# A fused attention and routed-FFN kernel: minima placed behind two-bank maxima, a unit's copy made in halves, attention rows split during the FFN, two late products evicted by ScalarE and GpSimd

## The chip, the cores and the metric

The kernel runs on one core of a Trainium2 chip. The core's engines run side by side, each with its own instruction queue worked off in order: TensorE (PE in the profile; PEld is its weight load) multiplies matrices into PSUM, VectorE (DVE) and ScalarE (ACT) read PSUM and work on it, GpSimd (POOL) works on SBUF, and SyncE (SP) issues nearly all DMA transfers of this kernel. They meet through semaphores only. The metric is the device time of one execution in microseconds; less is better. A verdict needs a difference that a few repeated runs can tell from none.

## The reference: what is computed

The input x has 2048 rows of 512 numbers. Two branches are mixed row by row by a gate:

```python
g = sigmoid((x * gate_w).sum(-1))
a = softmax_attention(x, wqkv, 32 heads of 16) @ wo
b = x, with a SwiGLU FFN added to the 2 rows that score highest in x @ w_r
out = g * a + (1 - g) * b
```

Nearly all the work is the attention: 32 heads, each with a 2048 x 2048 table of scores, its row maximum, its exponentials and its product with V.

## The kernel before: how the work is laid out

**Units and steps.** The attention is cut into 32 units (`UNITS`). A unit is a pair of heads and half of the queries; the last four units take a quarter of the queries of four heads. A unit has 16 steps (`KT`), one for each 128 keys, so there are 512 steps (`STEPS`). A step has four score pieces (`s_piece`, L655): a matmul with the transposed scores into one of three `st` banks of PSUM, and an exponential on ScalarE (L663) into `P`. Two steps later `av_mm` (L665) multiplies `P` with V and adds it up over the 16 steps in the one bank `av`. At the end of a unit `av_out` (L677) copies that bank to SBUF with one ScalarE instruction (L684; for a few units of the end with VectorE, L682) and SyncE sends the rows on.

**Maxima.** Before a unit's scores are exponentiated, the row maxima are needed. `m_piece` (L576) computes the scores once more, with queries as rows, 64 pieces to a unit (`EL`), in groups of three: two pieces fill the two-bank tile `mxa`, the third fills the one-bank tile `mxb`. VectorE reduces `mxa` with one instruction after the second piece (`r == 1`) and `mxb` with one after the third (`r == 2`), both at L590, into negated maxima `Mr`. A unit's 64 pieces do not divide by three, so units end at different places of a group: unit u ends behind a one-bank reduction if u % 3 is 2, behind a two-bank one if u % 3 is 1, and inside a two-bank tile if u % 3 is 0. At the end `m_unit` (L631) takes the minimum of the negated maxima on VectorE (L633) and splits it into a high and a low part on GpSimd (`pool_split`, L76); at the next two-bank reduction `m_rows` (L645) transposes the result on VectorE (L648) and sends it into rows 48 and 49 of the query tile `Qx` with eight small DMAs (L653). The score matmul of the unit then subtracts the maximum by itself. The maxima run 21 steps (`LEAD`) ahead of the exponentials, so a unit's rows are complete about five steps before its first step.

**The order is written out by hand.** One round of the loop (L954 to L973) walks the string `ORDER`, `sssmmA smssmmA msssmmf smssmmAm`: 12 score pieces (three steps), 12 pieces of maxima, three products with V (`A`) and one slot `f` for other work. The round thus has four groups of three pieces of maxima, called segments here: each has one two-bank and one one-bank reduction. `A` counts the steps; as it starts at -2 and a round has three, a unit ends on the third A of a round if u % 3 is 0, on the first if it is 1, on the second if it is 2.

**Other work.** The generator `slots` (L840) fills the `f` slots: the projections of the later heads, the FFN (`ff_in`, `ff_t`, `ff_down`, `ff_sum`), and the output projection with `wo` in three parts: `wo_groups((0, 1), (2,))`, `wo_groups((2,))` and `wo_last` (L564), one slot for each of 16 row tiles t or two. What a slot leaves in the one PSUM bank `fl` is evicted by a function put into the list `late`; `run_late` (L196) runs that list at the start of the next round. For the output projection it is `acc_add` (L471): ScalarE scales the bank into a tile `w` (L474) and GpSimd adds that to the accumulator (L475). `wo_last`, called one slot each for t = 12 to 15 with 64 rows (`k`) and then for t = 0 to 8 with 128, does not use the list: `finish` (L557) does both on VectorE with one instruction (L559), and `store` (L561) sends complete row tiles out. `at_step(s, ...)` puts a call at the end of step s; `gaps` holds small VectorE work, one item of which follows a two-bank reduction when neither `turn` nor anything else is due there.

**Attention rows for the output projection.** `load_at` (L491) reads 256 attention rows back with their reciprocal sums, `split_at` (L498) multiplies and splits them on GpSimd (six instructions for two groups of heads). The first such load stands behind `ff_sum`, and `wait(s + 8)` (L834, L879) leaves `f` slots empty until eight steps later. `load_acc` (L462) brings the residual x back from DRAM behind the scatter of the FFN's rows (L453), and `acc_scale` (L467) multiplies it by 1 - g on GpSimd.

**The end.** The round loop ends when the maxima are complete, with step 491. The 21 steps left run in a plain loop (L974 to L982) with one fill after each product with V. In it, `l_unit` (L729), called at the ends of steps 500 and 503, normalises the rows of unit 30: a reciprocal on VectorE (L733), a store to and a broadcast load from DRAM (L734, L736), a multiplication and the split (`split_last`, L541); `wo_last(8, 128)` waits for step 505 and needs that result of unit 30. After it comes `tail` (L754).

Of the kernel before, what the change touches and what calls it, by code (L numbers as in the profile page):

```python
# [36 lines left out]
def gated_mix(ctx: ExitStack, tc: tile.TileContext, xT, x, wqkv, wo, w_rg, w_gate, w_up, w_down,  # L37
# [526 lines left out]
    def wo_last(t, k):  # L564
        half, tt = divmod(t, 8)
        ah, al = lastp[half]
        ps = fl_tile()
        wo_terms(ps, ah[:k], al[:k], 3, slice(tt * 128, tt * 128 + 128), True, True)
        finish(t, ps)
        if k == 128:  # L570
            store(t)

# [3 lines left out]
    def m_piece(g):  # L576

        u, e = divmod(g, EL)
        t, c, j = e // 8, e // 2 % 4, e % 2
        r = g % 3  # L580
        if r == 0:
            MX[0] = mxa_tile()
        elif r == 2:
            MX[1] = mxb_tile()
        dst = MX[0][:, r] if r < 2 else MX[1]
        nc.tensor.matmul(dst, Qx[u % 3][64 * j:64 * j + 48, t * 128:t * 128 + 128],  # L586
                         k_of(u, t // 4)[64 * j:64 * j + 48, c * 512:c * 512 + 512], start=True, stop=True)
        if r:
            g0 = (g - 1 if r == 1 else g) % (3 * EL)
            nc.vector.tensor_reduce(Mr[:, g0:g0 + (2 if r == 1 else 1)], MX[r - 1], axis=AX.X, op=OP.max, negate=True)  # L590
            if r == 1:

                if turn:
                    m_rows(*turn.pop())
                elif e > 1 and e < EL - 1 and gaps:
                    gaps.pop(0)()
            if e == EL - 1 or (e == 0 and r == 1 and g):
                m_unit(u if e else u - 1)
                if u == UNITS - 1 and e:
                    m_rows(*turn.pop())  # L600
# [39 lines left out]
            pool_split(hl[:, :, 0], hl[:, :, 1], m)  # L640
        turn.append((u, hl))

    turn, gaps = [], []

    def m_rows(u, hl):  # L645

# [8 lines left out]
    def s_piece(s, j, c):  # L655
        u, kt = divmod(s, KT)
        if s not in P:
            P[s] = ring.tile([128, 4, 512], F32, tag="P", name="P", bufs=3)
        k = k_of(u, c)[64 * j:64 * j + 50, kt * 128:kt * 128 + 128]
        q = Qx[u % 3][64 * j:64 * j + 50, c * 512:c * 512 + 512]  # L660
        ps = mxb_tile() if s > STEPS - LEAD and c == 1 and j == 0 else st_tile()
        nc.tensor.matmul(ps, k, q, start=True, stop=True)  # L662
        nc.scalar.activation(P[s][:, 2 * j + c, :], ps, AF.Exp)  # L663

    def av_mm(s):  # L665
        u, kt = divmod(s, KT)
# [8 lines left out]
    Lt = {}  # L675

    def av_out(u):  # L677
        pair, half = divmod(u, 2)
        g, pp = divmod(pair, 4)
        o = o_tile("o", [128, 512])  # L680
        if STEPS > u * KT + KT + 2 > STEPS - LEAD:
            nc.vector.tensor_copy(o, AV[0])  # L682
        else:
            nc.scalar.activation(o, AV[0], AF.Copy)  # L684
        if u >= QU:
            AV[u] = o
            if u == UNITS - 1:
# [113 lines left out]
    def at_step(s, f, *a):  # L801
        fill.setdefault(s, []).append((f, a))
# [37 lines left out]
    def slots():  # L840
# [23 lines left out]
        at_step(now[0] + 3, load_wo)  # L864
        for c in range(4):
            at_step(now[0] + 6 + c, split_wo, c)
        yield
        yield
        yield from ff_down()
# [1 line left out]
        last_tiles()  # L871
        s = now[0]
        for nb in range(4):
            at_step(s + 5 + 2 * nb, load_acc, nb)
        for t in range(16):
            at_step(s + 11 + t, acc_scale, t)
        at_step(s + 1, load_at, 0, (0, 1))
        at_step(s + 4, split_at, 0, (0, 1))
        yield from wait(s + 8)  # L879
        yield from wo_groups((0, 1), (2,))  # L880
        assert now[0] > 3 * 8 * KT + 16
        yield from wo_groups((2,))
# [69 lines left out]
    count["m"] = 4 * LEAD  # L952

    while count["m"] < UNITS * EL:  # L954
        run_late()
        for o in ORDER:
            if o == "s":
                s, i = divmod(count["s"], 4)
# [8 lines left out]
            elif o == "A":  # L967
                if count["A"] < 0:
                    parts_next(2)
                p_v(count["A"])  # L970
                count["A"] += 1
            else:
                next(fills, None)  # L973
    for s in range(count["s"] // 4, STEPS + 2):  # L974
# [45 lines left out]
```

## Time and profile before

| what | value |
|---|---|
| median of 3 runs | 1425.82 us (1425.69 to 1426.97) |
| the profiled execution: time, span | 1426.34 us, 1424.4 us |
| granted TensorE clock | 0.999 |
| VectorE busy | 1292.2 us (91%), 1534 instructions |
| ScalarE busy | 1169.2 us (82%), 2264 instructions |
| GpSimd busy | 318.5 us (22%), 335 instructions |
| DMA | 92.87 MB, mean 65 GB/s |
| exponentials (L663, from `st`) | 2028, 1064.3 us, 599 ns each |
| maxima (L590) | 655 two-bank of 1216 ns, 654 one-bank of 689 ns |
| minima (L633) | 32 of 220 ns |
| copies of a unit (L684) | 31 of 600 ns |
| `finish` (L559), loop and tail | 18 of about 750 ns |
| `acc_add` (L474, L475) | 34 of about 700 ns and 1282 ns |

The span is the time from the first to the last instruction in the trace; the execution's own time has 1.9 us around it. A line of the timeline has the start in us, the duration in us, the engine, the line of the code, the operation and its tiles; in brackets stands how long the engine was idle before, and what ended that. Instructions on one engine overlap by some hundredths of a microsecond, so that starts, not durations, tell the pace.

### The profile page before, as it was taken

The page shows a single profiled execution, that of the slowest core. Times are in us where ns is not written, and L with a number is a line of the kernel's source. Part 1 is how long each engine was busy: PE and PEld are TensorE (multiplying, and loading weights), DVE is VectorE, ACT ScalarE, POOL GpSimd, SP SyncE. Part 2 cuts the span into 40 slices and gives each one's busy share as a digit, 9 for nine tenths or more (in the row PEclk, how much of TensorE's full clock was granted, in tenths as well). Part 3 has the DMA queues.
Part 4 walks back from the last instruction along what each step waited for, and adds up shares of the span by engine and source line. Part 5 has one row for each costly group of instructions (what it writes and reads, how often), then busy time and mean ns, then how long its engine had stood idle before and what let it go on. Part 6 is the DMA issues. An engine that isn't in the chain of part 4 may idle for free.

```text
span 1424.4 us, 24160 instructions
## 1 busy us (share of the span) xinstructions
PE 1416.3 (99%) x9113; PEld 627.8 (44%) x9113; DVE 1292.2 (91%) x1534; ACT 1169.2 (82%) x2264; POOL 318.5 (22%) x335
## 2 busy tenths in 40 slices
PE   9999999999999999999999999999999999999998
PEld 6654444444444444444444443434444444444433
DVE  6889999999999999999999999999999999999942
ACT  5568888888888888888888888888888888888886
POOL 4851101102000001200000100032742322234501
PEclk9999999999999999999999999999999999999999
DMA  8601121212123121312222332414313031012012
GB/s 245 230 27 51 31 40 31 68 31 52 46 67 92 62 53 32 67 31 67 55 83 53 100 87 69 103 40 129 83 31 68 22 76 37 14 31 58 17 49 79
DMA packets 51592, 92.87 MB, mean 65 GB/s; under 512 B 14208, under 2 KB 21376, under 8 KB 49844
## 3 DMA queue, kind: packets, MB, share of 16 engines
q1 hardware_dynamic: 51188, 91.02, 24.1%
q8 instruction: 72, 1.18, 0.3%
q0 software_dynamic: 288, 0.30, 0.1%
q14 instruction: 44, 0.36, 0.1%
HBM read 63.77 MB, written 28.57 MB: 65 GB/s over the span
## 4 chain that ended last, share of the span: by engine, by line
PE 99%; DMA 0%; ACT 0%; DVE 0%; SPq 0%; issue 0%; DVEq 0%; ACTq 0%
PE av L671 36%; PE st L662 24%; PE mxa L586 12%; PE mxb L586 10%; PE fl L154 6%; PE fl L508 4%; PE st L298 3%; PE st L154 2%; PE mxa L617 1%; PE fl L399 1%; DMA xs<-xT 0%; PE fl L437 0%; PE mxb L662 0%; DVE acc L559 0%; ACT P L663 0%; PE mxa L508 0%
## 5 line engine op out<-in xcount | busy, mean ns | idle before, releaser
L663 ACT ACTIVATE P<-st 128x512 f32<-128x512 f32 x2028 | 1064.3, 599 | 199.1 <-PE st L662 109.9
L590 DVE TENSOR_REDUCE Mr<-mxa 128x2 f32<-128x1024 f32 x655 | 796.6, 1216 | 3.3 <-PE mxa L586 2.5
L671 PE MATMUL av<-P,V 128*32 128x512 f32 x4096 | 545.3, 604 | 0.0
L662 PE MATMUL st<-Qx,Kx 50*128 50x512 f32 x2028 | 538.1, 444 | 1.3 <-ACT P L663 1.1
L590 DVE TENSOR_REDUCE Mr<-mxb 128x1 f32<-128x512 f32 x654 | 450.9, 689 | 62.1 <-PE st L662 21.7
L662 PEld LDWEIGHTS st<-Qx,Kx 50*128 50x128 f32 x2028 | 276.5, 184 | 233.6 <-ACT P L663 214.6
L586 PE MATMUL mxb<-Kx,Qx 48*128 48x512 f32 x654 | 325.3, 497 | 0.0
L586 PE MATMUL mxa<-Kx,Qx 48*128 48x512 f32 x1310 | 295.8, 417 | 0.0
L586 PEld LDWEIGHTS mxb<-Kx,Qx 48*128 48x128 f32 x654 | 119.5, 183 | 273.7 <-DVE Mr L590 271.2
L586 PEld LDWEIGHTS mxa<-Kx,Qx 48*128 48x128 f32 x1310 | 124.9, 183 | 46.4 <-DVE Mr L590 5.4
L671 PEld LDWEIGHTS av<-P,V 128*32 128x32 f32 x4096 | 81.1, 108 | 141.3 <-issue 135.2
L77 POOL TENSOR_SCALAR hl<-m 128x16 fp32r<-128x16 f32 x31 | 7.9, 254 | 435.3 <-DVE m L633 435.3
L205 POOL TENSOR_SCALAR ev<-pe 128x512 fp32r<-128x512 f32 x24 | 35.8, 1492 | 299.0 <-ACT pe L203 299.0
L475 POOL TENSOR_TENSOR acc<-acc,w 128x512 f32<-128x512 f32 x34 | 43.6, 1282 | 187.6 <-ACT w L474 173.5
L154 PE MATMUL fl<-xh,wh 128*128 128x512 f32 x96 | 42.9, 447 | 0.0
L154 PE MATMUL fl<-xh,wl 128*128 128x512 f32 x96 | 40.4, 421 | 0.0
L508 PE MATMUL fl<-woh,ahl 128*128 128x512 f32 x96 | 35.1, 447 | 0.0
L622 DVE TENSOR_REDUCE Mr<-mxa 128x2 f32<-128x1024 f32 x21 | 25.7, 1224 | 8.4 <-PE mxa L617 8.4
L154 PE MATMUL fl<-xl,wh 128*128 128x512 f32 x96 | 32.6, 421 | 0.0
L300 ACT ACTIVATE V<-st 128x512 f32<-128x512 f32 x16 | 9.6, 600 | 27.7 <-PE st L298 27.7
L206 POOL TENSOR_TENSOR ev<-pe,ev 128x512 fp32r<-128x512 f32 x24 | 30.8, 1285 | 2.0
L559 DVE SCALAR_TENSOR_TENSOR acc<-fl,gg,acc 128x512 f32<-128x512 f32 x13 | 9.7, 748 | 20.1 <-PE fl L508 17.8
(190 smaller groups left out, 778.6 us busy)
## 6 DMA issues: line engine op xcount, KB each, us to landing
q_scr<-ev SPq DMA_DIRECT2D x15, 512.0 KB
Kx<-k_scr SPq DMA_DIRECT2D x30, 256.0 KB
Qx<-q_scr SPq DMA_DIRECT2D x54, 128.0 KB
k_scr<-ev SPq DMA_DIRECT2D x13, 512.0 KB
Qx<-q_scr SPq DMA_DIRECT2D x70, 64.0 KB
xs<-xT SPq DMA_DIRECT2D x16, 256.0 KB
xn<-x SPq DMA_DIRECT2D x4, 1024.0 KB
Qx<-hr SPq DMA_DIRECT2D x256, 2.0 KB
```

The lines of the kernel that those rows point to most:

```text
L154: nc.tensor.matmul(ps, a[:, i, c, :], b[nb][:, c, :], start=n == 0, stop=n == 11)
L205: nc.gpsimd.tensor_scalar(ev[:, 0], t, 1.0, None, op0=OP.mult)
L206: nc.gpsimd.tensor_sub(ev[:, 1], t, ev[:, 0].bitcast(F32))
L298: nc.tensor.matmul(ps, a[nb][:, c, sl], b[:, c, :], start=c == 0 and n == 0, stop=c == 3 and n == 2)
L475: nc.gpsimd.tensor_add(a, a, w)
L508: nc.tensor.matmul(ps, a[:, sl], b[:a.shape[0], c, :], start=first and n == 0, stop=last and n == 2)
L586: nc.tensor.matmul(dst, Qx[u % 3][64 * j:64 * j + 48, t * 128:t * 128 + 128], k_of(u, t // 4)[64 * j:64 * j + 48, c * 512:c * 512 + 512], ...
L590: nc.vector.tensor_reduce(Mr[:, g0:g0 + (2 if r == 1 else 1)], MX[r - 1], axis=AX.X, op=OP.max, negate=True)
L622: nc.vector.tensor_reduce(*r, axis=AX.X, op=OP.max, negate=True)
L662: nc.tensor.matmul(ps, k, q, start=True, stop=True)
L663: nc.scalar.activation(P[s][:, 2 * j + c, :], ps, AF.Exp)
L671: nc.tensor.matmul(AV[0][32 * ct:32 * ct + 32, :], V[:, kt, h * VW:h * VW + 32], P[s][:, ct, :], start=kt == 0, stop=kt == KT - 1)
```

## The change

- **Minima.** In units that end behind a one-bank reduction (u % 3 is 2) `m_unit` is no longer called at once: the unit's number goes into a new list `due`, and `m_unit` runs behind the next two-bank reduction, two pieces later. `m_rows` then falls on the two-bank reduction after that. These are units 2, 5, ..., 29, ten of them.
- **Copy in halves.** For units that end on the second A of a round (u % 3 is 2, the same ten units) `av_out` copies 256 columns at once, and `o_half` the other 256 after the third exponential that follows. The DMAs of the unit's rows (`o_rows`, the old second part of `av_out`) are issued behind the second half.
- **Held evictions.** In the ten rounds that begin just after the end of a unit (u % 3 is 0), `run_late` runs behind the round's first A instead of at its start.
- **Attention rows during the FFN.** The first `load_at` and `split_at` stand between `ff_t(1)` and `ff_down`, at the fifth and the tenth step after the former. The wait of eight steps is gone, so the output projection starts two rounds earlier and all later fills move up by two slots; `load_acc` and `acc_scale` are placed anew behind `ff_sum`.
- **Late products.** `wo_last` puts `acc_add` into `late` as long as the step is below 490, and uses `finish` from then on. With the fills two slots earlier, `wo_last` for t = 12 and 13 falls on steps 485 and 488, and t = 14 on step 491.

```diff
@@ wo_last
-        finish(t, ps)
+        if now[0] < STEPS - LEAD - 1:
+            late.append((acc_add, (t, ps, gg)))
+        else:
+            finish(t, ps)
         if k == 128:
             store(t)
@@ m_piece
             if r == 1:
 
-                if turn:
+                if due:
+                    m_unit(due.pop())
+                elif turn:
                     m_rows(*turn.pop())
                 elif e > 1 and e < EL - 1 and gaps:
                     gaps.pop(0)()
-            if e == EL - 1 or (e == 0 and r == 1 and g):
+            if e == EL - 1 and r == 2 and u < UNITS - 1:
+                due.append(u)
+            elif e == EL - 1 or (e == 0 and r == 1 and g):
                 m_unit(u if e else u - 1)
@@
-    turn, gaps = [], []
+    due, turn, gaps = [], [], []
@@ s_piece
         nc.scalar.activation(P[s][:, 2 * j + c, :], ps, AF.Exp)
+        o_half()
@@ av_out
     def av_out(u):
-        pair, half = divmod(u, 2)
-        g, pp = divmod(pair, 4)
         o = o_tile("o", [128, 512])
         if STEPS > u * KT + KT + 2 > STEPS - LEAD:
             nc.vector.tensor_copy(o, AV[0])
+        elif STEPS - LEAD > u * KT + KT + 2 and u % 3 == 2:
+            nc.scalar.activation(o[:, :256], AV[0][:, :256], AF.Copy)
+            half_o.append([3, u, o, AV[0]])
+            return
         else:
             nc.scalar.activation(o, AV[0], AF.Copy)
+        o_rows(u, o)
+
+    half_o = []
+
+    def o_half():
+
+        if half_o:
+            half_o[0][0] -= 1
+            if not half_o[0][0]:
+                _, u, o, ps = half_o.pop()
+                nc.scalar.activation(o[:, 256:], ps[:, 256:], AF.Copy)
+                o_rows(u, o)
+
+    def o_rows(u, o):
+        pair, half = divmod(u, 2)
+        g, pp = divmod(pair, 4)
         if u >= QU:
@@ slots
         at_step(now[0] + 3, load_wo)
         for c in range(4):
             at_step(now[0] + 6 + c, split_wo, c)
+        at_step(now[0] + 5, load_at, 0, (0, 1))
+        at_step(now[0] + 10, split_at, 0, (0, 1))
         yield
         yield
         yield from ff_down()
@@
         s = now[0]
         for nb in range(4):
-            at_step(s + 5 + 2 * nb, load_acc, nb)
+            at_step(s + 3 + 3 * nb, load_acc, nb)
         for t in range(16):
-            at_step(s + 11 + t, acc_scale, t)
-        at_step(s + 1, load_at, 0, (0, 1))
-        at_step(s + 4, split_at, 0, (0, 1))
-        yield from wait(s + 8)
+            at_step(s + 6 + t, acc_scale, t)
+        yield
         yield from wo_groups((0, 1), (2,))
@@ the loop
     while count["m"] < UNITS * EL:
-        run_late()
+        hold = count["A"] % KT == 0 and count["A"] > 0
+        if not hold:
+            run_late()
         for o in ORDER:
...
                 p_v(count["A"])
                 count["A"] += 1
+                if hold:
+                    hold = False
+                    run_late()
             else:
                 next(fills, None)
```

## The prediction

> **What bounds the kernel now.** I read the busy times first, then the chain of waits.
>
> ```profile
> PE 1416.3 (99%) x9113; PEld 627.8 (44%) x9113; DVE 1292.2 (91%) x1534; ACT 1169.2 (82%) x2264; POOL 318.5 (22%) x335
> PE 99%; DMA 0%; ACT 0%; DVE 0%; SPq 0%; issue 0%; DVEq 0%; ACTq 0%
> ```
>
> TensorE looks full, but the ends of its matmuls are modelled and a late matmul stays "busy". So neither view tells whether an edit on another engine is worth anything. What does is the pace of the loop, and for that I took VectorE's timeline and measured from the start of one two-bank reduction to the start of the one four segments (a round, three steps) later.
>
> ```profile
> 97.86 1.23 DVE L590 TENSOR_REDUCE Mr<-mxa 128x2 f32<-128x1024 f32 x1 [0.30 <-PE mxa L586]
> ...
> 113.37 1.21 DVE L590 TENSOR_REDUCE Mr<-mxa 128x2 f32<-128x1024 f32 x1
> ...
> 121.08 1.22 DVE L590 TENSOR_REDUCE Mr<-mxa 128x2 f32<-128x1024 f32 x1
> 122.33 0.22 DVE L633 TENSOR_REDUCE m<-Mr 128x16 f32<-128x64 f32 x1
> ...
> 136.53 1.22 DVE L590 TENSOR_REDUCE Mr<-mxa 128x2 f32<-128x1024 f32 x1
> ...
> 159.80 1.22 DVE L590 TENSOR_REDUCE Mr<-mxa 128x2 f32<-128x1024 f32 x1
> ...
> 163.77 0.22 DVE L633 TENSOR_REDUCE m<-Mr 128x16 f32<-128x64 f32 x1
> ...
> 175.46 1.22 DVE L590 TENSOR_REDUCE Mr<-mxa 128x2 f32<-128x1024 f32 x1
> ...
> 1360.65 1.22 DVE L590 TENSOR_REDUCE Mr<-mxa 128x2 f32<-128x1024 f32 x1
> ```
>
> A quiet round takes 121.08 - 113.37 = 7.71 us. The first and the last row are 652 segments, 163 rounds apart: (1360.65 - 97.86) / 163 = 7.747. So everything that ends of units, evictions and fills cost the whole loop beyond its quiet pace is about 163 x 0.037 = 6 us. That is the ceiling for the loop's three edits, before anything has been worked out: 0.4% of the time. The loop is a tight ring: VectorE frees `mxa`, TensorE fills it and goes on to the product with V, ScalarE frees `st`. Only what delays that ring costs time.
>
> **The minima.** The rows show both places. Unit 1's minimum (122.33) follows a two-bank reduction: the two rounds from 121.08 to 136.53 take 15.45, against 2 x 7.71 = 15.42 quiet, so 0.03 us. Unit 2's (163.77) follows a one-bank reduction and holds up the two-bank one behind it: 159.80 to 175.46 is 15.66, 0.24 us over quiet. The difference has a reason: behind a two-bank reduction the next thing on VectorE is `mxb`, which TensorE fills late anyway. Ten units move from the dear place to the cheap one, but to another segment of the round than unit 1's, and their transpose falls one segment later too; I take 0.19 rather than 0.21 each: **-1.9 us** (bounds: -2.4, all of it; -0.9, if the new segment has less room). Behind the moved minimum are queued on VectorE the next reduction, and on GpSimd the split; the latter now stands behind the GpSimd work of an eviction of the same round in some units, and the transpose waits for it. One segment of 1.9 us lies between minimum and transpose, the split takes half a microsecond.
>
> **The copy in halves.**
>
> ```profile
> 220.89 0.60 ACT L684 ACTIVATE o<-av 128x512 f32<-128x512 f32 x1
> 221.38 3.20 ACT L663 ACTIVATE P<-st 128x512 f32<-128x512 f32 x6
> ...
> 221.84 1.21 DVE L590 TENSOR_REDUCE Mr<-mxa 128x2 f32<-128x1024 f32 x1
> ...
> 229.64 1.22 DVE L590 TENSOR_REDUCE Mr<-mxa 128x2 f32<-128x1024 f32 x1
> ...
> L774 ACT ACTIVATE rxl<-rl x1: 418/418/418, 1413.8 to 1413.8; 128x256 f32<-128x256 f32 x1
> ```
>
> Unit 2's copy (220.89) is followed by six exponentials without a gap, so ScalarE runs late there; the round from 221.84 to 229.64 takes 7.80, 0.09 over quiet. Halves spread the delay over two segments. But a copy of half the columns costs 0.42, not 0.30, by the only row of that size, so ten units cost ScalarE up to 10 x (2 x 0.42 - 0.60) = 2.4 us more. ScalarE is no bound over the round (82% busy), so I take half of what there is to gain: **-0.5 us** (bounds -0.9, +2.4). The bank `av` comes free some 2 us later; the next unit's first product with V is two segments of 1.9 away, and waits for nothing if that holds. A rule speaks against this edit: the Trainium skill, "ScalarE: Activation LUTs", section "What ACT_TABLE_LOAD costs", has an ACTIVATE at a fixed 186 ns plus 0.833 ns a column, of which 93 ns overlap with its neighbour. By it a second instruction costs 0.09 us each time, 0.9 us in ten units (an estimate); were all of that on the path, the term would be +0.4 and the time 1424.0. The rows agree with the rule's order of size: 0.42 for 256 columns.
>
> **The held evictions.** A hold matters only where the list is not empty in one of the ten rounds. Counting slots, that is two rounds: one of the FFN, and one of the last `wo_groups`, which leaves work in every round.
>
> ```profile
> 883.09 0.19 ACT L419 ACTIVATE gu<-fl 112x32 f32<-112x32 f32 x1
> ...
> 1251.58 1.22 DVE L590 TENSOR_REDUCE Mr<-mxa 128x2 f32<-128x1024 f32 x1
> ...
> 1254.48 0.60 ACT L684 ACTIVATE o<-av 128x512 f32<-128x512 f32 x1
> 1254.98 0.68 ACT L474 ACTIVATE w<-fl,gg 128x512 f32<-128x512 f32 x1
> ...
> 1259.98 1.22 DVE L590 TENSOR_REDUCE Mr<-mxa 128x2 f32<-128x1024 f32 x1
> ```
>
> At 1254.48 and 1254.98 copy and eviction stand back to back, and the round takes 8.40, 0.69 over quiet: the largest single loss of the loop. With one group of exponentials between them I leave 0.1 of it: -0.6. The FFN's eviction of 0.19 us is worth 0.1 at most. **-0.7 us** (bounds -0.9, 0). Behind the held eviction waits the next use of the bank `fl`, two groups later.
>
> **The late products.** In the loop two rounds' `wo_last` take the place of two `wo_part`, with the same eviction (about 0.7 us on ScalarE, then GpSimd), so they cost nothing there. Two rounds earlier on, two slots that were empty are now filled. What can gain is the end, which has two fills fewer: t = 13 and 14.
>
> ```profile
> 1363.79 1.07 PE L671 MATMUL av<-P,V 128*32 128x512 f32 x8
> ...
> 1370.92 1.07 PE L671 MATMUL av<-P,V 128*32 128x512 f32 x8
> ...
> 1386.39 0.24 DVE L733 RECIPROCAL Ls<-Ls 128x16 f32<-128x16 f32 x1
> ...
> 1386.94 1.76 SPq L734 DMA_DIRECT2D l_scr<-Ls  x1
> ...
> 1390.19 0.63 SPq L736 DMA_DIRECT2D rb<-l_scr  x1
> ...
> 1391.39 1.06 PE L671 MATMUL av<-P,V 128*32 128x512 f32 x8
> ...
> 1393.80 1.07 PE L671 MATMUL av<-P,V 128*32 128x512 f32 x8
> ...
> 1394.37 0.69 DVE L740 TENSOR_TENSOR an<-an,rb 64x512 f32<-64x512 f32 x1 [2.78 <-DMA rb<-l_scr]
> ...
> 1395.60 1.28 POOL L553 TENSOR_TENSOR lahl<-an,lahl 128x512 fp32r<-128x512 f32 x1 [32.83 <-DVE lahl L552]
> 1395.76 1.07 PE L671 MATMUL av<-P,V 128*32 128x512 f32 x8
> 1396.76 0.74 PE L508 MATMUL fl<-woh,lahl 128*128 128x512 f32 x2
> ```
>
> Three steps with a 64-row fill take (1370.92 - 1363.79) / 3 = 2.38 each, eight with a 128-row fill (1391.39 - 1370.92) / 8 = 2.56, the first without one 2.41, the next 1.96. Two 64-row steps that become empty ones save 2 x (2.38 - 1.97) = 0.8. But `wo_last(8)` hangs on unit 30's rows, a chain that does not start earlier: the reciprocal behind the ninth fill (1386.39), the store (1386.94), the load (1390.19), the product (1394.37), the split, done at 1395.60 + 1.28 = 1396.88. Its first matmul starts at 1396.76 and its second, which needs the split, about 0.34 later: the chain is hidden by some 0.2 us only. After the change the nine fills of the end are one of 64 rows and eight of 128, so the ninth comes 2 x (2.56 - 2.38) = 0.4 later, and the split is done at about 1397.3, while TensorE would be there at 1396.3. So the saved 0.8 turns into a wait of 1.0 and the end comes **+0.25 us** later (bounds: -0.8, if the chain is shorter than I read it; +0.5).
>
> **The FFN stretch.**
>
> ```profile
> 943.88 1.28 POOL L78 TENSOR_TENSOR wol<-wos,woh 128x512 fp32r<-128x512 f32 x1
> ...
> 950.87 0.20 DVE L648 STREAM_TRANSPOSE hr<-hl 128x32 f32<-128x32 f32 x1
> ...
> 973.73 0.72 POOL L502 TENSOR_TENSOR ats<-ats 128x256 f32<-128x256 f32 x1 [2.50 <-PE mxb L586]
> ...
> 977.93 0.74 POOL L78 TENSOR_TENSOR ahl<-ats,ahl 128x256 fp32r<-128x256 f32 x1
> ```
>
> GpSimd is done with `wo` at 945.16; `split_at` now follows there. Its six instructions stand from 973.73 to 977.93 + 0.74 now, 4.9 us, so it ends at 950.1, and unit 21's split of half a microsecond after it at 950.6, just ahead of the transpose of 950.87. The moved loads are issued where SyncE's queue has run ahead; `acc_scale` now comes before unit 22's split on GpSimd, whose transpose would be the next to be late. **+0.1 us** (bounds 0, +0.6: one late transpose).
>
> **The sum:** -1.9 - 0.5 - 0.7 + 0.25 + 0.1 = -2.75. The profiled execution took 1426.34 (1.9 around its span), which gives 1423.6; the median of the runs is 0.52 lower, which gives **1423.1**.
>
> **The rivals.**
>
> *The end gives its 0.8 too.* For it: the chain's links are DMA latencies (3.3 and 4.2 us between their rows), and SyncE's queue ahead of them changes. Against it: the reciprocal follows the ninth fill on VectorE in order. -2.75 - 0.25 - 0.8 = -3.8: 1422.0.
>
> *The losses move on instead of vanishing.* The minimum and the second half of the copy stay on their engines, one segment later. For it: the quiet segments leave only a tenth or two of a microsecond. Against it: unit 1's 0.03. Then only the hold and the end count, -0.45: 1425.4.
>
> *The rows of the maxima come too late: slower.*
>
> ```profile
> 165.27 5.29 SPq L653 DMA_DIRECT2D Qx<-hr  x8
> ...
> 174.32 0.74 PE L662 MATMUL st<-Qx,Kx 50*128 50x512 f32 x3
> ...
> 415.73 5.29 SPq L653 DMA_DIRECT2D Qx<-hr  x8
> ...
> 423.88 0.50 PE L662 MATMUL st<-Qx,Kx 50*128 50x512 f32 x1
> ```
>
> Unit 2's eight DMAs are issued from 165.27 on, its first score matmul is the third of those at 174.32, its second, which needs the last four DMAs, leads the next group, a segment of 1.9 us later, at 176.2. Three pieces later means that the DMAs go out from 167.2 to 172.5, 3.7 us ahead of it. If a DMA lands later than that, TensorE waits in ten units, and each 0.6 us of it costs 6: -2.75 + 6 = +3.2, 1429.0. Against it: unit 8's were issued from 415.73 and left 423.88 - 421.02 = 2.9 us, without a loss.
>
> *The change doesn't do what it says* in its last part: only two products leave VectorE, since t = 14 is already at step 491. That is in the sum.
>
> **Chances.** The forecast 0.45, the end's gain 0.28, losses that move 0.17, late rows 0.10. A difference of 0.2% (2.85 us) is about what a measurement of this kernel can tell from no change. The forecast lies just inside it, so half of its chance and the second case are faster: 0.50; the other half, and the third case, 0.41; late rows 0.09. The range leaves out the late rows and the outer half of the copy's bounds: 1421.0 to 1426.2.
>
> **What would show it.** Right: the two rounds around units 2, 5, ..., 29 take 15.45 instead of 15.66, the round at 1251.6 some 7.8, and `wo_last(8)`'s second matmul waits for GpSimd. Wrong: a wait of the transpose for GpSimd or of TensorE for `Qx` at ends of units, products with V waiting for the second half, exponentials without gaps for more than six, or VectorE's pace between units off 7.71.

## The result, and the profile after

| | before | after |
|---|---|---|
| median of 10 runs each | 1426.11 us (1425.09 to 1427.09) | 1422.15 us (1421.11 to 1423.06) |
| ratio | 1 | 0.9974, 95% interval 0.9966 to 0.9982 |
| profiled execution: time, span | 1426.34, 1424.4 us | 1422.2, 1420.2 us |

The medians differ by 3.96 us, 0.28% of the time before, and the interval of the ratio leaves out 1. The first question is where in the span it lies. The page of the profile after answers as little as the one before did: TensorE 4 us less busy, VectorE 3, ScalarE 2 more.

```profile
PE 1412.3 (99%) x9113; PEld 630.1 (44%) x9113; DVE 1289.3 (91%) x1532; ACT 1170.9 (82%) x2276; POOL 320.3 (23%) x337
PE 95%; DMA 2%; POOL 1%; DVE 1%; SPq 0%; ACT 0%; issue 0%; POOLq 0%; DVEq 0%; ACTq 0%
```

The timeline of after answers it. Its columns are start, duration, engine, line, operation and tiles; the reductions moved from L590 to L593, the minimum is L640, the copy L690 and L705 (halves) or L694 (whole).

```profile
97.41 1.23 DVE L593 TENSOR_REDUCE Mr<-mxa 128x2 f32<-128x1024 f32 x1 [0.31 <-PE mxa L589]
...
159.31 1.22 DVE L593 TENSOR_REDUCE Mr<-mxa 128x2 f32<-128x1024 f32 x1
...
163.16 1.22 DVE L593 TENSOR_REDUCE Mr<-mxa 128x2 f32<-128x1024 f32 x1
164.29 0.21 DVE L640 TENSOR_REDUCE m<-Mr 128x16 f32<-128x64 f32 x1
164.49 0.69 DVE L593 TENSOR_REDUCE Mr<-mxb 128x1 f32<-128x512 f32 x1
...
174.70 1.22 DVE L593 TENSOR_REDUCE Mr<-mxa 128x2 f32<-128x1024 f32 x1
...
221.11 1.21 DVE L593 TENSOR_REDUCE Mr<-mxa 128x2 f32<-128x1024 f32 x1
...
228.81 1.21 DVE L593 TENSOR_REDUCE Mr<-mxa 128x2 f32<-128x1024 f32 x1
...
1248.85 1.21 DVE L593 TENSOR_REDUCE Mr<-mxa 128x2 f32<-128x1024 f32 x1
...
1256.68 1.22 DVE L593 TENSOR_REDUCE Mr<-mxa 128x2 f32<-128x1024 f32 x1
...
1357.09 1.22 DVE L593 TENSOR_REDUCE Mr<-mxa 128x2 f32<-128x1024 f32 x1
```

The first and the last row cut the span into three, as 97.86 and 1360.65 did before:

| stretch of the profiled execution | before | after | difference |
|---|---|---|---|
| start to the first of these reductions | 97.86 | 97.41 | -0.45 |
| the 163 rounds | 1262.79 | 1259.68 | -3.11 |
| from the last one to the end of the span | 63.75 | 63.11 | -0.64 |

The change does not touch the first stretch. Over the fourteen kernels of this study it lay between 97.0 and 99.1, a spread larger than what most edits are worth. So below an edit is read from the other two stretches, and the runs' medians only bear it out. The rounds that no edit touches also differ, by up to 0.45 us in sum from one execution to another, while a single round repeats to about 0.03; so the safest reading of an edit is the length of the very rounds in which it stands.

Inside the rounds the edits show where they were put. Two rounds around unit 2 take 174.70 - 159.31 = 15.39 instead of 15.66. The round of unit 2's copy takes 228.81 - 221.11 = 7.70 instead of 7.80. The round of the held eviction takes 1256.68 - 1248.85 = 7.83 instead of 8.40. ScalarE's timeline shows the last two: groups of three exponentials now stand between what stood back to back.

```profile
220.16 0.39 ACT L690 ACTIVATE o<-av 128x256 f32<-128x256 f32 x1
220.54 1.58 ACT L670 ACTIVATE P<-st 128x512 f32<-128x512 f32 x3
221.99 0.41 ACT L705 ACTIVATE o<-av 128x256 f32<-128x256 f32 x1
...
1251.75 0.60 ACT L694 ACTIVATE o<-av 128x512 f32<-128x512 f32 x1
1252.24 1.57 ACT L670 ACTIVATE P<-st 128x512 f32<-128x512 f32 x3
1253.67 0.71 ACT L474 ACTIVATE w<-fl,gg 128x512 f32<-128x512 f32 x1
```

Summed over the rounds in which they stand: minima -2.2, halves -0.8, held evictions -0.55 (0.56 and 0.07 gained in two rounds, 0.08 given back in the round behind the first). One more round gives back 0.35, that of unit 21 in the FFN stretch.

```profile
932.17 1.49 POOL L77 TENSOR_SCALAR woh<-wos 128x512 fp32r<-128x512 f32 x1 [4.43 <-DMA wos<-wo]
...
943.46 0.74 POOL L502 TENSOR_TENSOR ats<-ats 128x256 f32<-128x256 f32 x1
...
948.70 0.22 POOL L78 TENSOR_TENSOR hl<-m,hl 128x16 fp32r<-128x16 f32 x1
948.95 0.21 DVE L655 STREAM_TRANSPOSE hr<-hl 128x32 f32<-128x32 f32 x1 [0.39 <-POOL hl L78]
```

GpSimd splits `wo` (L77, L78), then the attention rows (from 943.46), then unit 21's minimum (948.70), and the transpose waits 0.39 us for that. In this execution GpSimd had idled 4.43 us until `wo` landed; in e4, where nothing waits, it was 3.82.

The end is what the prediction did not expect. These rows answer to those shown of before:

```profile
1383.22 0.24 DVE L759 RECIPROCAL Ls<-Ls 128x16 f32<-128x16 f32 x1
1383.77 1.08 SPq L760 DMA_DIRECT2D l_scr<-Ls  x1
1386.22 0.62 SPq L762 DMA_DIRECT2D rb<-l_scr  x1
1390.02 0.69 DVE L766 TENSOR_TENSOR an<-an,rb 64x512 f32<-64x512 f32 x1 [6.55 <-DMA rb<-l_scr]
1391.24 1.28 POOL L553 TENSOR_TENSOR lahl<-an,lahl 128x512 fp32r<-128x512 f32 x1 [32.05 <-DVE lahl L552]
1392.55 0.73 PE L508 MATMUL fl<-woh,lahl 128*128 128x512 f32 x2
```

The two matmuls of `wo_last(8)` run without a gap. The split is done at 1391.24 + 1.28 = 1392.52, 0.37 us ahead of the second, which starts some 0.34 behind 1392.55. From the store's issue to the end of the split the chain takes 8.75 us; before it took 1396.88 - 1386.94 = 9.94.

### The profile page after: what moved, and what is told of

Its sections match the earlier page's. It is cut to its first block, busy times and chain, and to the rows that moved or that the text cites. A ratio compares the mean times of both kernels' runs of the same rounds, so it can differ in the third digit from the quotient of the medians.

```text
span 1420.2 us, 24172 instructions
## 1 busy us (share of the span) xinstructions
PE 1412.3 (99%) x9113; PEld 630.1 (44%) x9113; DVE 1289.3 (91%) x1532; ACT 1170.9 (82%) x2276; POOL 320.3 (23%) x337
## 4 chain that ended last, share of the span: by engine, by line
PE 95%; DMA 2%; POOL 1%; DVE 1%; SPq 0%; ACT 0%; issue 0%; POOLq 0%; DVEq 0%; ACTq 0%
PE av L679 35%; PE st L669 23%; PE mxa L589 12%; PE mxb L589 10%; PE fl L154 6%; PE fl L508 4%; PE st L298 3%; DMA xs<-xT 1%; PE mxa L624 1%; DMA wvs<-wqkv 1%; PE fl L399 1%; PE st L154 0%; POOL woh L77 0%; DMA wos<-wo 0%; PE mxb L669 0%; POOL wol L78 0%
## 5 line engine op out<-in xcount | busy, mean ns | idle before, releaser
L593 DVE TENSOR_REDUCE Mr<-mxa 128x2 f32<-128x1024 f32 x655 | 796.1, 1215 | 2.7 <-PE mxa L589 2.5
L593 DVE TENSOR_REDUCE Mr<-mxb 128x1 f32<-128x512 f32 x654 | 451.0, 690 | 61.0 <-PE st L669 18.0
L77 POOL TENSOR_SCALAR hl<-m 128x16 fp32r<-128x16 f32 x31 | 7.8, 252 | 294.5 <-DVE m L640 294.5
L298 PE MATMUL st<-Kx,xh 128*128 128x512 f32 x64 | 27.6, 431 | 0.0
```

The lines of the kernel that those rows point to most:

```text
L298: nc.tensor.matmul(ps, a[nb][:, c, sl], b[:, c, :], start=c == 0 and n == 0, stop=c == 3 and n == 2)
```

## The experiments

Each difference of "the loop" and "the end" below is that of the second or third stretch of the table, against before for the single parts and against the changed kernel for its variants. Medians are in us. The runs of before beside the first four had a median of 1426.14, those beside the next three 1425.79, beside e8 to e10 1425.55, beside the last two 1426.5.

### One part alone

**e1, the minima** (kernel before plus the list `due`):

```diff
+                if due:
+                    m_unit(due.pop())
-                if turn:
+                elif turn:
...
+            if e == EL - 1 and r == 2 and u < UNITS - 1:
+                due.append(u)
-            if e == EL - 1 or (e == 0 and r == 1 and g):
+            elif e == EL - 1 or (e == 0 and r == 1 and g):
```

> The kernel before with the moved minima alone (units 2, 5, ..., 29). Theory (a minimum behind a two-bank reduction hides under the late filling of the one-bank tile): each of the ten unit ends gains about 0.21 us in the pace of the maxima, 2.1 us in all, about 1424.0. Rival (the delay moves on one segment later): no gain, 1426.1.

Measured: 1423.65, ratio 0.9982 (0.9973 to 0.9991); the loop -2.48, the ten places -0.17 to -0.25 each, 2.2 in all; the end 63.79, unchanged. The theory holds.

**e2, the copy in halves** (`o_half`, `o_rows` and the branch in `av_out` alone):

```diff
+        elif STEPS - LEAD > u * KT + KT + 2 and u % 3 == 2:
+            nc.scalar.activation(o[:, :256], AV[0][:, :256], AF.Copy)
+            half_o.append([3, u, o, AV[0]])
+            return
```

> The kernel before with the copy in halves alone. Theory (the delay of the exponentials is spread over two segments and absorbed): the round after the ten copies goes from 7.80 to about 7.71, 0.5 to 0.9 us in all, about 1425.4. Rival by the price of a second instruction on ScalarE (0.09 to 0.24 us each): 0.9 to 2.4 us slower, 1427 to 1428.5.

Measured: 1425.28, ratio 0.9994 (0.9985 to 1.0003), too little for the medians, as the interval holds 1. In the trace the loop is -0.82; the ten rounds are 0.04 to 0.13 shorter, 0.9 in all, and one other is 0.26 longer. The price rule had the edit as a loss: it is none.

**e3, the hold** (the loop's `hold` alone):

```diff
-        run_late()
+        hold = count["A"] % KT == 0 and count["A"] > 0
+        if not hold:
+            run_late()
...
+                if hold:
+                    hold = False
+                    run_late()
```

> The kernel before with the held evictions alone. Theory (only the two rounds with something in the list matter): the round of 8.40 us becomes about 7.8, the FFN's round gains up to 0.1, the rest is untouched: 0.7 us in all, about 1425.4. Rival (the eviction is as late behind the first product as before it): no gain, 1426.1.

Measured: 1425.0, ratio 0.9993 (0.9984 to 1.0002), again too little for the medians. In the trace one round of the last heads is 0.56 shorter (its first and last reduction are shown, 7.84 apart instead of 8.40), the round behind it 0.09 longer, and one of the FFN 0.08 shorter: 0.55 in all. The loop is -0.73; the rest stands in rounds that the edit does not touch.

```profile
1251.52 1.21 DVE L590 TENSOR_REDUCE Mr<-mxa 128x2 f32<-128x1024 f32 x1
...
1259.36 1.23 DVE L590 TENSOR_REDUCE Mr<-mxa 128x2 f32<-128x1024 f32 x1
```

**e4, the fills** (attention rows during the FFN, the wait gone, late products through `late`):

```diff
+        at_step(now[0] + 5, load_at, 0, (0, 1))
+        at_step(now[0] + 10, split_at, 0, (0, 1))
...
-        yield from wait(s + 8)
+        yield
```

> The kernel before with the earlier attention rows, the removed wait and the late products alone. Theory now (two 64-row fills of the end turn into empty steps, and the chain through DRAM to the last-but-one product stays hidden): the end from the last two-bank reduction on takes 63.1 instead of 63.75 us, and the transpose of unit 21 waits for GpSimd, 0.4 us: 0.25 us faster in all, 1425.9. Rival of the prediction (the chain binds): the end takes 64.0, 0.65 us slower in all, 1426.7.

Measured: 1425.12, ratio 0.9992 (0.9983 to 1.0001), too little for the medians; in the trace the end takes 63.15 against 63.75, so the whole gain of the end belongs to this part. The chain of unit 30, in the timeline of e4:

```profile
1386.24 1.09 SPq L737 DMA_DIRECT2D l_scr<-Ls  x1
1388.70 0.62 SPq L739 DMA_DIRECT2D rb<-l_scr  x1
...
1392.45 0.69 DVE L743 TENSOR_TENSOR an<-an,rb 64x512 f32<-64x512 f32 x1 [6.51 <-DMA rb<-l_scr]
1393.68 1.28 POOL L553 TENSOR_TENSOR lahl<-an,lahl 128x512 fp32r<-128x512 f32 x1 [32.02 <-DVE lahl L552]
```

Store to end of split is 1394.96 - 1386.24 = 8.72, as in the changed kernel. From the store's issue to the load's it is 2.46, from there to the product 3.75. Before it was 3.25 and 4.18. In e1 to e3, whose fills are those of before, the first link was 2.95, 3.02 and 2.45, the second about 4.15. So the first link varies from one execution to the next, and the second goes with the fills. All fourteen profiles say so: the second link takes 4.14 to 4.22 in the four with the old fills and 3.38 to 3.80 in the ten with the new ones. In the timelines of the four, two stores are issued between the load and the product; in those of the ten, none. That these stores are the cause was not tried. Unit 21's transpose did not wait in this execution.

### The end of the chain

**e8, one more hop** for unit 30's reciprocals:

```diff
+            i = u - QU
+            if u == UNITS - 2:
+                nc.sync.dma_start(l_scr[3], l_scr[i])
+                i = 3
```

> The changed kernel with one more hop through DRAM (8 KB copied from one scratch tensor to another) between the store and the load of unit 30's sums, since the step-later run did not move the chain in time. Theory (the chain ends 0.2 to 0.6 us ahead of the second matmul that needs it): the hop adds 2.5 to 3.3 us by the store's own link, TensorE waits for all but that margin, and the end from the last two-bank reduction on goes from 63.1 to 65.3 or more, about 1424.5. Rival (ample room): 63.1, 1422.15.

Measured: 1423.59, ratio 0.9984 (0.9975 to 0.9994); the end 65.1 against 63.11, all 2 us of it (65.3 or more was expected). In the timeline of e8 the matmul now waits for GpSimd, which the prediction had expected of the change itself:

```profile
1392.55 0.50 PE L508 MATMUL fl<-woh,lahl 128*128 128x512 f32 x1 [0.82 <-DVE lahl L552]
1392.58 1.27 POOL L553 TENSOR_TENSOR lahl<-an,lahl 128x512 fp32r<-128x512 f32 x1 [34.27 <-DVE lahl L552]
1393.90 0.50 PE L508 MATMUL fl<-woh,lahl 128*128 128x512 f32 x1 [0.84 <-POOL lahl L553]
```

So the chain does lie right behind the path: it was shorter than predicted, not unimportant.

**e6, the chain one step later** (`l_unit(30, 0)` at s + 4 instead of s + 3):

```diff
-            at_step(s + 3, l_unit, u, 0)
+            at_step(s + (4 if u == UNITS - 2 else 3), l_unit, u, 0)
```

> The changed kernel with unit 30's reciprocal, store and load one step later. Theory (the chain through DRAM ends 0.37 us ahead of the second matmul of the product that needs it, so a step of 2 us more makes it bind): TensorE waits there and the end from the last two-bank reduction on takes 1.6 us more, 64.7 instead of 63.1, about 1423.8. Rival (the chain has ample room): the end stays at 63.1, 1422.15.

Measured: 1421.58, ratio 0.997 (0.9959 to 0.9981), the end 63.13. The edit did not do what it was to do: the store is issued 26.68 us behind the last two-bank reduction in both kernels, since the reciprocal stands behind the same VectorE work either way. It says nothing on the chain. It says something on unit 21: with the same code there, its transpose did not wait.

### The FFN stretch

**e5, the split later** (`split_at` three steps later, behind unit 21's split on GpSimd):

```diff
-        at_step(now[0] + 10, split_at, 0, (0, 1))
+        at_step(now[0] + 13, split_at, 0, (0, 1))
```

> The changed kernel with the first split of the attention rows at the thirteenth instead of the tenth step, behind unit 21's minimum. Theory (unit 21's transpose waits for GpSimd, which still works on that split): the two rounds around it lose their 0.46 us, about 1421.7, and nothing else moves. Rival (the loss comes from the load's traffic or from VectorE): the rounds stay as long, 1422.15.

Measured: 1421.65 (1421.38 to 1422.23), ratio 0.9971 (0.996 to 0.9982); the round of unit 21 is 0.36 shorter than in the changed kernel. But e6 and e8, with the split and unit 21's minimum unmoved, are 0.36 and 0.34 shorter there too. What decides is when `wo` lands. GpSimd idles 4.43 us for it in the changed kernel and 4.36 in e9. From the start of its split of `wo` to unit 21's minimum it is then 946.58 - 932.17 = 14.41 and 14.46, and there the transpose waits, 0.39 and 0.34. In e4, e6, e8, e10, e11 and e12 GpSimd idles 3.74 to 3.88, the distance is 14.93 to 15.06, and nothing waits. (In e7 unit 21's minimum itself was moved.) e5 takes that chance away; that its median beats the changed kernel's is not shown, the intervals overlap.

### The copy

**e9, the whole copy late** (behind the third exponential, not halved):

```diff
-            nc.scalar.activation(o[:, :256], AV[0][:, :256], AF.Copy)
...
-                nc.scalar.activation(o[:, 256:], ps[:, 256:], AF.Copy)
+                nc.scalar.activation(o, ps, AF.Copy)
```

> The changed kernel with the ten copies not halved but made whole, behind the third exponential, where the second half stood. Theory (the delay has to be spread over two segments): the exponentials behind it start up to 0.3 us late or the next product with V waits for the bank, 0.05 to 0.1 us in each of ten units, 0.5 to 1 us in all, about 1423. Rival (it is enough to leave the segment without a product with V, which has the least room on ScalarE): no difference, 1422.15.

Measured: 1422.85, ratio 0.9979 (0.997 to 0.9989). In the trace the ten rounds take 0.7 more than in the changed kernel, up to 0.14 each, and only 0.08 less than before. So the theory holds: of the 0.8 that the halves gain in these rounds, 0.7 is the halving and no more than 0.1 the later place. (The whole loop is only 0.40 longer, since other rounds differ the other way.)

### Why a minimum costs what it costs

The prediction's reason was the place: dear behind a one-bank reduction, cheap behind a two-bank one. Four variants of the changed kernel test it. "Cost of an end" is here the length of eight segments around a minimum, less the usual length of such segments (the median of each of the four kinds in that execution). The mean over units 2, 5, ..., 29 is 0.23 us before and 0.02 after, over units 1, 4, ..., 28 it is 0.01 and 0.02. Where the eight segments begin shifts single figures by some hundredths.

**e7, the minima of units 3, 6, ..., 30 one two-bank reduction later:**

```diff
-            elif e == EL - 1 or (e == 0 and r == 1 and g):
+            elif e == 0 and r == 1 and g:
+                due.append(u - 1)
+            elif e == EL - 1:
```

> The changed kernel with the minima of units 3, 6, ..., 30 also one two-bank reduction later, so that they fall on the segment in which those of units 1, 4, ... lie. Theory (what a minimum costs depends on how late the one-bank tile of its segment is filled): the ten unit ends go from 0.06 to 0.2 us over quiet to about 0.03, 0.8 us in all, about 1421.3. Rival (what is left at these ends doesn't come from the minimum): no gain, 1422.15.

Measured: 1421.44, ratio 0.997 (0.9959 to 0.998); those ten ends cost 0.04 to 0.19 as before the edit (unit 21's wait apart), and one 0.26. The rival holds: what is left there is not from the minimum. What it is from was not found. The median is the one that the theory asked for, but e5 and e6, run beside it without this edit, have medians as low.

**e10, the minima of units 1, 4, ..., 28 behind the one-bank reduction that follows:**

```diff
+            if r == 2 and due1:
+                m_unit(due1.pop())
...
+            elif e == EL - 1 and r == 1 and u < UNITS - 1:
+                due1.append(u)
```

> The changed kernel with the minima of units 1, 4, ..., 28, so far behind a two-bank reduction at 0.03 us each, put behind the one-bank reduction that follows, with the transposes where they were. Theory (the place behind a one-bank reduction is the dear one, whatever the unit): each of these ten ends costs 0.2 us more, 2 us in all, about 1424.2. Rival (the cost belonged to the units 2, 5, ... and their segment): less than 0.5 us, 1422.4.

Measured: 1426.53 (1423.84 to 1428.72), ratio 1.0003 (0.9993 to 1.0012). Nine of the ten ends cost 0.00 to 0.05, no more than in the changed kernel: the place behind a one-bank reduction is not dear in every segment, and the prediction's reason, taken alone, falls. The move also took the minimum away from the reduction whose result it reads; that this matters shows in e12. The tenth end, unit 22, costs 7 us by another way, told below.

**e11, the minima of units 2, 5, ..., 29 behind the next one-bank reduction:**

```diff
-                if due:
-                    m_unit(due.pop())
-                elif turn:
+                if turn:
...
+            if e == 2 and r == 2 and due:
+                m_unit(due.pop())
```

> The changed kernel, with the minima of units 2, 5, ..., 29 behind the one-bank reduction of the next segment instead of behind the two-bank reduction before it; their transposes stay. First theory (what a 0.2 us instruction costs is what it delays the following reduction beyond that segment's slack): the two-bank reduction that it now delays has some 0.15 us of slack against a delay of 0.26, so at most 0.1 us at each of ten ends, 0 to 1 us in all, 1422 to 1423. Second theory (the place behind a one-bank reduction is dear by itself): 0.2 us each, 2 us in all, about 1424. Rival (place means nothing): 0, 1422.

Measured: 1422.44, ratio 0.9973 (0.9962 to 0.9984). The ends cost 0.10 on average against 0.02, and the ten rounds in which these minima stand take 0.6 more than in the changed kernel, 0.06 each: inside the first theory's bound. The loop is only 0.05 longer, but unit 21's transpose did not wait here, which gives back 0.36.

**e12, the minima of units 1, 4, ..., 28 without 22 at the very place that units 2, 5, ..., 29 left:**

```diff
+            if e == 3 and r == 2 and due1:
+                m_unit(due1.pop())
...
+            elif e == EL - 1 and r == 1 and u < UNITS - 1 and u != 22:
+                due1.append(u)
```

> The changed kernel, with the minima of units 1, 4, ..., 28 without 22 two reductions later: behind the one-bank reduction of the last segment of their round, the very place at which the kernel before had the minima of units 2, 5, ..., 29. First theory (the place costs, since the reductions that follow there have the least slack): nine unit ends dearer by some 0.2 us, 1.9 us in all, about 1424.0. Rival (the cost belonged to units 2, 5, ..., 29 and what else they have there): the nine ends as in the changed kernel, within 0.05 us, 1422.2.

Measured: 1429.13 (1425.86 to 1430.68), ratio 1.0013 (1.0003 to 1.0022), slower than both expectations; in the profiled execution that is by two late ends told below. The nine ends themselves (for units 1 and 4, read before their rows are late) cost 0.08 on average against 0.02, and the nine rounds in which these minima stand are 0.08 longer each, where the place had cost 0.22 a round in the kernel before. Both expectations miss: neither the place alone nor the units alone make the price. The timelines show what else differs. Before, unit 2, with the minimum's row (163.77, 0.22) between these two:

```profile
163.04 0.69 DVE L590 TENSOR_REDUCE Mr<-mxb 128x1 f32<-128x512 f32 x1 [0.18 <-PE st L662]
...
163.91 1.22 DVE L590 TENSOR_REDUCE Mr<-mxa 128x2 f32<-128x1024 f32 x1
```

e12, unit 1:

```profile
124.65 0.69 DVE L593 TENSOR_REDUCE Mr<-mxb 128x1 f32<-128x512 f32 x1 [0.20 <-PE st L673]
125.26 0.21 DVE L644 TENSOR_REDUCE m<-Mr 128x16 f32<-128x64 f32 x1
125.39 1.21 DVE L593 TENSOR_REDUCE Mr<-mxa 128x2 f32<-128x1024 f32 x1
```

In the quiet loop a two-bank reduction starts 0.61 behind the one-bank one. With a minimum between them it is 163.91 - 163.04 = 0.87 before, but 125.39 - 124.65 = 0.74 in e12. The minimum starts 0.73 behind the reduction in the one and 0.61 in the other. The difference that these rows show: before, the minimum of unit 2 read the maximum that the instruction just ahead of it had written; in e12 that maximum is three reductions old (the move is by three, not by two as the expectation has it). The same step stands behind two-bank reductions: a minimum that reads its forerunner's result starts 1.25 behind it (unit 1, before: 122.33 - 121.08), one that doesn't 1.13 (after, unit 2: 164.29 - 163.16). So a minimum takes 0.13 us of VectorE, and 0.12 more if it hangs on the instruction ahead of it. How much of that TensorE feels depends on the segment: 0.22 of the 0.26 before, 0.08 of the 0.13 at the same place in e12, 0.06 of the 0.13 in e11, nothing measurable in e10 nor behind unit 2's two-bank reduction in the changed kernel, where `mxb` comes late anyway. One slack of some 0.05 us at the old place (an estimate from these figures: 0.26 - 0.22 and 0.13 - 0.08) gives both its prices, so nothing else of the units 2, 5, ..., 29 is needed. No run moved the dependence alone, with unit and place held; so that split of the price is worked out, not tried.

## Why the prediction was right, and where it was wrong

The forecast of 1423.1 is 0.95 us above the measured median, inside its range, and the time is that of its first rival (1422.0), in which the end gives its gain too. A part of the closeness is luck: the gain was forecast as 2.75 and measured as 3.96, and the forecast started from a median of three runs that lay 0.29 below the 1426.11 of the ten. Of its three signs of being right, two came (15.39 and 7.83); the third, `wo_last(8)`'s second matmul waiting for GpSimd, did not. Of its signs of being wrong one came, at one place: a transpose waiting for GpSimd, at unit 21.

| term | forecast | measured in the profiled execution of after | alone |
|---|---|---|---|
| minima | -1.9 | -2.2 | -2.2 (e1) |
| halves | -0.5 | -0.8 | -0.9 (e2) |
| held evictions | -0.7 | -0.55 | -0.55 (e3) |
| late products, the end | +0.25 | -0.64 | -0.60 (e4) |
| FFN stretch | +0.1 | +0.35 | none (e4) |

**The step that failed is the chain of unit 30.** (By the forecast's own figures, 0.8 saved and a wait of 1.0, the term is +0.2 rather than +0.25.) Its parts came out one by one: the ninth fill is later, by 26.13 - 25.74 = 0.4 us counted from the last two-bank reduction to the reciprocal, as forecast; TensorE saves its 0.8 and is at the second matmul 1392.89 - 1357.09 = 35.80 us behind that reduction, where the forecast had 1396.3 - 1360.65 = 35.65. Wrong was the length, taken over from before as if fixed: 9.9 us in the one execution that was at hand, 8.75 after and 8.72 in e4. The prediction had named these links as DMA latencies that might change and given that 0.28, then let one sample decide. Four profiles with the old fills, before and e1 to e3, range from 9.18 to 9.94: before was the longest of them. With 9.18, the split would have been done some 0.25 us after TensorE is there instead of 1.0, and the term would have been -0.55. The rest came with the change: in the nine profiles with the new fills and no extra hop the chain takes 8.32 to 8.89, shorter than any of the four. So the wait that the forecast set against the saved 0.8 did not come: the first link happened to be long in the one profile of before, and the second is shorter in every profile with the new fills.

**The minima: right in size, in part right in their reason.** The forecast took "behind a two-bank reduction" as what makes the cheap place. By e12 a third of the old price, 0.08 of 0.22, was the place, in that the reduction behind it has little slack. The rest goes with the minimum hanging on the instruction just ahead of it, which moving it by one reduction cured on the way. One of the prediction's own pairs of rows had it (1.25 behind a reduction of 1.22, where reductions overlap by some hundredths as a rule), and it was not read.

**The copy in halves** gained within its bounds, 0.8 against 0.9 at most. The halves take 0.39 and 0.41 us, 0.20 more than one whole, so about 2.0 us of ScalarE in ten units, near the 2.4 that was feared, and no loss from it shows. By the Trainium skill's "ScalarE: Activation LUTs", section "What ACT_TABLE_LOAD costs", the estimate was 0.9 us. Even the measured 2.0 is not seen in the pace: nine of the ten rounds take 7.70 to 7.72, that of a quiet round.

**The held evictions** gained what was left between the forecast's rounds (7.8 forecast, 7.83 measured); the 0.08 that the next round gives back was not in the forecast.

**The FFN stretch** was forecast with 0.1 and a bound of 0.6, with the place and the waiting instruction named: unit 21's transpose behind `split_at`. In the profiled execution it did wait, 0.39; in e4, e6, e8 and e10 to e12 it did not, with `split_at` at the same place. The step taken as fixed, the time at which GpSimd is done with `wo`, hangs on a DMA.

**Losses that move on:** the places into which minima and halves moved cost 0.02 at the ends of units and nothing visible at the copies. The rival falls.

**Late rows:** in the changed kernel no score matmul waits for `Qx`. The mechanism is real and was met in e12. There the rows of units 1 and 4 were issued behind a store that waited for GpSimd on SyncE's queue:

```profile
128.98 0.38 SPq L191 DMA_DIRECT2D k_scr<-ev  x1
129.46 5.33 SPq L664 DMA_DIRECT2D Qx<-hr  x8
...
136.00 0.47 PE L673 MATMUL st<-Qx,Kx 50*128 50x512 f32 x1 [1.45 <-DMA Qx<-hr]
```

The eight transfers are issued until 134.79 and the score matmul goes 1.2 us later, after an idle 1.45: that round took 1.88 longer. So from the end of the last issue to the use it takes 1.2 us, not the 2.9 that the prediction knew to be enough. In the changed kernel unit 1's rows went out from 123.96, ahead of that store. The later minimum was just enough to fall behind it.

## What to carry to other kernels

Place a small instruction that reads a result one instruction later than the one that made it, and ahead of work that is late anyway; read both from start-to-start times, not from durations. Where a chain of DMAs is hidden by a few tenths, its length in one profile is one sample: price the edit at both ends of the spread of several profiles before letting the wait decide the sign, and note which other transfers the edit moves to or from its queue. Before moving an issue, look for what it falls behind on its queue, for there a step of one or two instructions costs nothing or microseconds.

## What the runs showed of the hardware that was not expected

**A short stall of TensorE can cost the clock.** In e10 unit 22's minimum, one reduction later, fell behind a `split_at` on GpSimd, and its transpose held up the reductions behind it. The view by stretches of e10 (length, then busy time and instructions of TensorE, weight loads, VectorE, ScalarE and GpSimd, then the granted clock, the share of the DMA engines and GB/s):

```profile
988.00:990.00 2.00, 2.00 (x15) 0.53 (x11) 0.11 (x1) 1.57 (x3) 1.82 (x4) 1.00 0.00 0
990.00:993.00 3.00, 0.83 (x5) 0.30 (x4) 1.97 (x4) 0.95 (x2) 2.92 (x5) 0.98 0.00 1
993.00:996.00 3.00, 3.00 (x12) 0.90 (x14) 1.77 (x2) 0.73 (x2) 3.00 (x3) 0.50 0.02 3
996.00:999.00 3.00, 3.00 (x11) 1.50 (x11) 1.92 (x2) 1.57 (x3) 1.16 (x1) 0.50 0.39 63
999.00:1002.00 3.00, 3.00 (x14) 0.77 (x14) 1.92 (x2) 2.15 (x4) 0.20 (x1) 0.50 0.76 291
1002.00:1005.00 3.00, 3.00 (x22) 1.48 (x20) 1.82 (x2) 1.57 (x3) 3.00 (x3) 0.82 0.08 33
```

```profile
991.03 0.21 DVE L659 STREAM_TRANSPOSE hr<-hl 128x32 f32<-128x32 f32 x1 [2.92 <-POOL hl L78]
```

TensorE idles 2.2 us, then the granted clock is 0.50 for 10.24 us (992.85 to 1003.09), and the end costs 7 us instead of the 2 of the stall. In e12 TensorE's wait of 1.36 us for unit 4's rows was followed by the same (clock 0.50 for 10.24 us from 261.59 on, 6 us lost), its wait of 1.45 us for unit 1's was not (1.9 lost). The runs of e10 bear it out: the two with a mean clock of 1.000 took 1423.84 and 1423.99, the four at 0.996 took 1427.91 to 1428.72. In e12 the mean clock does not sort the runs so well (1429.83 at 0.999, 1426.98 at 0.998); what else differs there is open.

Why the shorter wait cost the clock and the longer one did not can be read from the traces. In all fourteen, the changes of the granted clock lie whole multiples of 3.413 us apart: 986.45, 10.24 and 423.25 in e10 are 289, 3 and 124 of them, 256.00, 10.24 and 1157.12 in e12 are 75, 3 and 339. Cut e12 at that raster:

```profile
131.89:135.30 3.41, 2.66 (x21) 0.94 (x17) 3.09 (x6) 2.61 (x6) 0.00 (x0) 1.00 0.02 3
135.30:138.71 3.41, 2.71 (x18) 1.12 (x19) 1.76 (x2) 1.24 (x4) 0.99 (x1) 1.00 0.16 58
258.18:261.59 3.41, 2.05 (x17) 0.62 (x14) 2.33 (x3) 2.51 (x5) 0.00 (x0) 1.00 0.02 3
261.59:265.00 3.41, 3.41 (x15) 1.00 (x17) 1.23 (x1) 0.60 (x1) 0.00 (x0) 0.50 0.98 190
```

Unit 1's wait falls across a boundary, 0.75 us of idle TensorE in one stretch and 0.70 in the next; unit 4's 1.36 lie in one stretch, at whose end the clock falls; so do 2.0 us of e10's stall (989.44 to 992.85). So what counts in these three stalls is the idle time within one such stretch, and the bound lies between 0.75 and 1.36 us. It is not a general one: at the end of the program stretches with 1.7 to 1.8 us of idle TensorE kept the clock (e3 from 1417.50, e10 from 1419.52). The Trainium skill, "TensorE: Matmul & The Clock Gate", section "What's actually happening", has the half clock after at least one idle window of about 3.4 us, counted by a free-running clock. The raster agrees with the window; that the window has to be idle does not, since 1.36 of its 3.41 us were enough here.

**A dependent instruction on VectorE starts 0.12 us later than an independent one**: 1.25 against 1.13 behind a two-bank reduction, 0.73 against 0.61 behind a one-bank one, the same to 0.01 in all fourteen traces, the first unit apart. The Trainium skill, "VectorE: DVE Perf Modes", section "The DRAIN you can't avoid", has eight copies with a semaphore behind each take as long as eight with one behind the last, and says of a next operation that is not held that it starts earlier. The second agrees with these rows; the first would let a wait for the forerunner cost nothing, and here it costs 0.12 us.
